# An attention and expert kernel: filler products on a program constant, score banks filled one behind the other, four value copies turned into transfers, two groups of transposes swapped

## The chip, the cores and the metric

The kernel runs on one core of a Trainium2 chip. The metric is the device time of one execution in microseconds. The engines are named as the profile names them: PE is TensorE (PEld its weight loads), DVE is VectorE, ACT is ScalarE, POOL is GpSimd, and SP is SyncE, which issues most of the transfers.

## The reference

```
q, k, v: (4, 8, 576, 64)
scores = q @ k^T / 8, masked to 0 <= query - key < 64; attention = softmax @ v
x = attention as (2304, 512)
logits = x @ w_gate + log1p(exp(x @ w_noise)) * noise; the two best of 8 experts, softmax weights
out = sum over the two of weight * (relu(x @ w1[e]) @ w2[e])        # w1 (8,512,1024), w2 (8,1024,512)
h = out @ w_in;  g = h if h >= 1, 0 if h <= -1, else (h + 1)^2 / 4;  result = g @ w_out
```

## The kernel before, in words

The program is one long sequence in an order written out by hand, and every engine takes its own instructions strictly in that order. Three parts follow one another: attention with routing (to about 104 us), the eight experts, and the second network. Only the first is touched.

Attention works on 18 tiles of 128 tokens. A tile i consists of two units, u = 2i and 2i + 1. Unit k of a tile uses rows 64k to 64k + 63 of the transposed queries and keys, which holds one head of each of four pairs. These are the pieces, by the names in the code:

- `A(i)` computes the scores of both units of tile i on TensorE: for each unit two mask products into the unit's bank (64x512, opening it), and eight score products (64x128), two for each of four head pairs. Unit u has bank `Sb[u % 3]`, unit 3 a bank of `OB`.
- `top(u)` takes the maximum of the scores on VectorE (a reduction of 128x512) and negates and scales it, on VectorE for u < 4 and on POOL behind that. `soft(u)` is four exponentials on ScalarE. `C(u)` transposes the result on TensorE, and ScalarE copies it out as `pt`.
- `Dm(u)`, for odd u, multiplies a whole tile with the values: 16 products, 64x65, of `vO[i]` and `vE[i]`, into `OB`. VectorE divides by the sums (`rl`, `x`), and SyncE stores the tile to `x_dram`.
- `Ex(i, u)` transposes tile i of `x`, and `logits` multiplies it with the gate's weights. `route(g)` for groups of 8, 4 and 6 tiles is a list of small VectorE operations that is played out in portions between the attention's own (`advance`), with one-hot rows (`ohr`, `ohe`) that `place` multiplies on TensorE.

`step(u)` for u = 0 to 36 puts them in order: loads, `A` of the tile after next (even u), `Ex`, `C(u)`, `top`, `soft`, `logits`, `place`, `advance`, `Dm(u - 1)`. The transposes of `C` and `Ex` take turns in two banks (`rot`). In step 34 before the change `C(34)` came ahead of `Ex(15, 34)`.

Two small overlaps between neighbours matter here. A tile's keys reach 64 tokens back: `load_qk(j)` loads queries and keys for a pair of tiles, keys into columns 64 to 319 of a buffer, and `keys_before(j)` copies the 64 before them, on POOL, from the pair before. The values do the same: `vO[i + 1]` is the buffer `vE[i]`, and after tile i's products its first 64 rows are overwritten with those of `vE[i + 1]`, by a POOL copy in `Dm` (L415).

At the very start TensorE fills the time until the first queries and keys are there: `open_ids` opens the bank in which the places of tokens are collected, and `warm(9)` makes nine products of 128x512 of the zero tile `wz`, which VectorE sets first. Four more follow behind the first scores.

All loads, and the stores of tiles, go through SyncE's one queue, in the order of the program.

Of the kernel before, what the change touches and what calls it, by code (L numbers as in the profile page):

```python
# [13 lines left out]
BF16 = mybir.dt.bfloat16  # L14
# [7 lines left out]
P = 128  # L22
# [6 lines left out]
NT = N // P  # L29
# [28 lines left out]
def fused_kernel(ctx, tc, qT, kT, v, wg, noise, wcat, out, wd=None):  # L58
    nc = tc.nc
# [26 lines left out]
    OB = att.enter_context(tc.tile_pool(name="pso", bufs=1, space=PS)).tile([P, 2, 512], F32, name="ob")  # L86


    kTv = kT.rearrange("(g p) t -> p g t", p=P)
    qTv = qT.rearrange("(g p) t -> p g t", p=P)  # L90
    k_t, vE, vO = {}, {}, {}
# [9 lines left out]
    def load_qk(j):  # L101
        q_t[j] = qbuf[:, j % 2]
        kt = k_t[j] = qk.tile([P, 4, 320], F32, tag="k", name=f"k{j}")

        for h in (slice(0, P), slice(P, 256)) if j == 0 else (slice(0, 256),):
            t = slice(256 * j + h.start, 256 * j + h.stop)
            nc.sync.dma_start(out=kt[:, :, 64 + h.start:64 + h.stop], in_=kTv[:, :, t])
            nc.sync.dma_start(out=q_t[j][:, :, h], in_=qTv[:, :, t])
        if j == 0:
            nc.vector.memset(kt[:, :, 0:64], 0.0)  # L110


    def keys_before(j):
        nc.gpsimd.tensor_copy(k_t[j][:, :, 0:64], k_t[j - 1][:, :, 256:320])
# [18 lines left out]
    def load_raw(n, eng=nc.sync):  # L133
        raws[n] = t = raw.tile([P, 1024], F32, tag="raw", name=f"raw{n}")
        if NF <= n < N2:

            if n % NF == 0:
                r = E - 2 if n >= NCE else (n // NF - 1) % (E - 2)
                dyn[n // NF] = nc.values_load(cnt_i[0:1, 1 + r:2 + r], engines=[mybir.EngineType.SP], min_val=0,
                                          max_val=(E - 1) * NF)  # L140
            eng.dma_start(out=t, in_=wcat[bass.ds(dyn[n // NF] + n % NF, 1)].rearrange("o p n -> (o p) n"))
        else:
            eng.dma_start(out=t, in_=wcat[n])
# [184 lines left out]
    NU = 2 * NT  # L328
# [6 lines left out]
    def rot(u):  # L335
        turn[0] += 1
        return bank[3 + 2 * (turn[0] % 2)] if u <= NU else bank[6]
# [6 lines left out]
    def score(u):  # L344
        return OB[:, 0, :] if u == 3 else Sb[u % 3]

    def A(i):
        j = i // 2
        qo, ko = (i % 2) * P, (i % 2) * P
        sb = [score(2 * i + k) for k in range(2)]  # L350
        for k in range(2):
            r = slice(64 * k, 64 * k + 64)
            for c in range(2):
                m = masks[c][int((2 * i + c) % 9 == 0)]
                nc.tensor.matmul(sb[k][64 * c:64 * c + 64, :], lhsT=id64[r, :],
                                 rhs=m[r].unsqueeze(1).to_broadcast([64, 4, P]), start=True, stop=False)
        for g in range(4):
            for c in range(2):
                for k in range(2):
                    r = slice(64 * k, 64 * k + 64)  # L360
                    keys = k_t[j][r, g, ko + 64 * c:ko + 64 * c + P]
                    if c == 0:
                        keys = keys.rearrange("p (s n) -> p s n", s=2)[:, ::-1, :]
                    nc.tensor.matmul(sb[k][64 * c:64 * c + 64, g * P:g * P + P],
                                     lhsT=q_t[j][r, g, qo + 64 * c:qo + 64 * c + 64],
                                     rhs=keys, start=False, stop=(g == 3))

    def top(u):
        mx = wk.tile([P, 4], F32, tag="mx", name=f"mx{u}", bufs=3)
        nb = wk.tile([P, 4], F32, tag="nb", name=f"nb{u}", bufs=3)  # L370
        nc.vector.tensor_reduce(out=mx, in_=score(u).rearrange("p (g n) -> p g n", g=4), axis=AX.X, op=ALU.max)

        (nc.vector if u < 4 else nc.gpsimd).tensor_scalar(out=nb, in0=mx, scalar1=-0.125, scalar2=None, op0=ALU.mult)
        mxs[u] = nb

    def soft(u):
        sb, nb = score(u), mxs.pop(u)
        p = wk.tile([P, 4, P], F32, tag="p", name=f"p{u}", bufs=4)
        for g in range(4):
            nc.scalar.activation(p[:, g, :], sb[:, g * P:g * P + P], AF.Exp, bias=nb[:, g:g + 1], scale=0.125)  # L380
        pr[u] = p

    def C(u):
        p = pr.pop(u)
        PTb = rot(u)
        for g in range(4):
            nc.tensor.transpose(PTb[:, g * P:g * P + P], p[:, g, :], idn)
        t = wk.tile([P, 512], F32, tag="pt", name=f"pt{u}", bufs=PTB)
        nc.scalar.activation(t, PTb, AF.Copy)
        pts[u] = t  # L390

    def Dm(u):
        i, r = divmod(u, 2)
        if r == 0:
            return
        ts = [pts.pop(2 * i + k) for k in range(2)]
        for h in range(H):
            g, k = divmod(h, 2)
            for c in range(2):
                vv = (vO, vE)[c][i]  # L400
                nc.tensor.matmul(OB[64 * c:64 * c + 64, h // 4, (h % 4) * VW:(h % 4) * VW + VW],
                                 lhsT=ts[k][:, g * P + 64 * c:g * P + 64 * c + 64], rhs=vv[:, h * VW:h * VW + VW],
                                 start=True, stop=True)
        ov = OB[:, :, 0:4 * VW].rearrange("p b (h d) -> p b h d", d=VW)
        rl = wk.tile([P, 2, 4, 1], F32, tag="rl", name=f"rl{i}")
        nc.vector.tensor_scalar(out=rl, in0=ov[:, :, :, D:VW], scalar1=1e-9, scalar2=None, op0=ALU.add)
        nc.vector.reciprocal(out=rl, in_=rl)
        x = wk.tile([P, H, D], F32, tag="x", name=f"x{i}", bufs=3)
        nc.vector.tensor_tensor(out=x.rearrange("p (b h) d -> p b h d", b=2), in0=ov[:, :, :, 0:D],
                                in1=rl.to_broadcast([P, 2, 4, D]), op=ALU.mult)  # L410
        xs[i] = x
        nc.sync.dma_start(out=x_dram[P * i:P * i + P, :], in_=x.rearrange("p h d -> p (h d)"))
        if i + 1 < NT:
            if i + 2 < NT:
                nc.gpsimd.tensor_copy(vE[i][0:64, :], vE[i + 1][0:64, :])  # L415
            vO[i + 1] = vE[i]

# [236 lines left out]
    def warm(n, to=OB[:, 1, :]):  # L654
        for _ in range(n):
            nc.tensor.matmul(to, lhsT=wz[:, 0:P], rhs=wz, start=True, stop=True)

    def open_ids():
        nc.tensor.matmul(IDS[:, 0:2 * NK], lhsT=wz[:, 0:P], rhs=wz[:, 0:2 * NK], start=True, stop=False)

    open_ids()
    warm(9)
    A(0)
    for u in range(2):
        top(u)
        soft(u)
    warm(4)

    def logits(i, u):
        Gm(i, u)  # L670
        g, t = tile_group[i]
        if t == GROUPS[g] - 1:
            live.append(route(g))
            next(live[-1])

    def step(u):
        for c in range(EW):
            if u == L0 + LS * c:
                load_raw(c)
        if u + 2 < NU:  # L680
            if (u + 2) % 4 == 0 and (u + 2) // 4 + 1 < NT // 2:
                load_qk((u + 2) // 4 + 1)
                keys_before((u + 2) // 4 + 1)
            if (u + 1) % 2 == 0 and (u + 1) // 2 + 1 < NT:
                load_v((u + 1) // 2 + 1)


        m = u // 2
        if u % 2 == 0:
            if u + 2 < NU:  # L690
                A(m + 1)
            if u == NU:
                nc.scalar.activation(vE[NT - 2][0:64, :], vE[NT - 1][0:64, :], AF.Copy)
            if u == NU - 2:
                C(u)
            if 0 <= m - 2 < NT:
                Ex(m - 2, u)
        if u < NU and u != NU - 2:
            C(u)
        if u % 2 == 0 and u + 2 < NU:  # L700
            top(u + 2)
            top(u + 3)
        if u + 2 < NU:
            soft(u + 2)

        if u % 2 == 1 and 0 <= m - 2 < NT:
            logits(m - 2, u)
        place()
        early()
        advance(MARKS[u > NU - 10])  # L710
        if 0 <= u - 1 < NU:
            Dm(u - 1)

        for c in range(EW):
            for h in range(2):
                if u == L0 + LS * c + 3 + h:
                    split_w(c, h)
                if u == L0 + LS * c + 4 + h and c < EW - 2:
                    rest_w(c, slice(512 * h, 512 * h + 512))
            if u == L0 + LS * c + 4 and EW <= c + 2 < NF:  # L720
                load_raw(c + 2)
# [694 lines left out]
    for q, (ui, p) in enumerate(items):  # L1416
# [5 lines left out]
        while ndone < len(items) and ndone <= q + (1 if items[ndone][0] == FIRST2 else 2):  # L1422
            i = items[ndone]
# [84 lines left out]
```

## Time and profile before

| | us |
|---|---|
| median of 3 runs | 947.14 (946.4 to 947.47) |
| the profiled execution, its time | 950.02 |
| its span (first to last instruction) | 948.3 |
| busy in it: TensorE | 935.7 |
| VectorE | 665.6 |
| ScalarE | 436.5 |
| POOL | 186.2 |

The profiled execution is one of its own and carries the profiler; its time is compared with its span, and differences with the median. Busy time is a share over stages of different kinds: which engine sets the pace of a stage is read from that stage.

### The profile page before, as it was taken

What the parts mean: (1) busy time and instruction counts of PE and PEld (TensorE: products, weight loads), DVE (VectorE), ACT (ScalarE), POOL (GpSimd) and SP (SyncE); (2) the same over time, 40 slices, a digit from 0 to 9 for tenths busy, and PEclk for the clock granted to TensorE, in tenths of its full rate; (3) what the DMA queues carried; (4) which work ended last, traced back from release to release, by engine and by line L of the source; (5) the groups of instructions that cost most, each with busy time, mean ns of one, the idle gap of its engine ahead of it and who ended that gap; (6) DMA issues with size and microseconds to landing.
All of it is one profiled execution on the core that took longest, in us unless ns stands there. A gap on an engine that the chain in (4) does not pass through costs nothing. (4 is left out here: it accounts for less than half of the span.)

```text
span 948.3 us, 17990 instructions
## 1 busy us (share of the span) xinstructions
PE 935.7 (99%) x6779; PEld 832.3 (88%) x6781; DVE 665.6 (70%) x1411; ACT 436.5 (46%) x907; POOL 186.2 (20%) x249
## 2 busy tenths in 40 slices
PE   9999999999999999999999999999999999999998
PEld 6887888988888989898888889988999899899986
DVE  4689765477997968889533366767867776687664
ACT  6898314345565555555433266333433333342221
POOL 3222013133645353354402030000000000000000
PEclk9999999999999999999999999999999999999999
DMA  8874136555888878767725566775576559556521
GB/s 258 300 252 167 56 100 186 188 191 199 290 288 275 261 236 277 257 206 260 252 89 184 204 231 236 252 256 178 177 256 213 164 174 308 175 178 213 182 95 44
DMA packets 91274, 196.95 MB, mean 208 GB/s; under 512 B 7320, under 2 KB 18072, under 8 KB 91184
## 3 DMA queue, kind: packets, MB, share of 16 engines
q1 hardware_dynamic: 83152, 171.68, 54.6%
q0 software_dynamic: 6736, 21.86, 6.4%
q10 hardware_dynamic: 1296, 2.23, 0.6%
q8 instruction: 54, 0.88, 0.4%
q14 instruction: 36, 0.29, 0.1%
HBM read 155.45 MB, written 40.29 MB: 206 GB/s over the span
## 5 line engine op out<-in xcount | busy, mean ns | idle before, releaser
L969 PE MATMUL bank<-wo,hall 128*128 128x512 f32 x864 | 237.6, 394 | 0.0
L969 PE MATMUL bank<-w,hall 128*128 128x512 f32 (+3 forms) x944 | 234.6, 396 | 0.1
L969 PEld LDWEIGHTS bank<-w,hall 128*128 128x128 f32 (+3 forms) x944 | 167.7, 183 | 35.2 <-issue 0.3
L969 PEld LDWEIGHTS bank<-wo,hall 128*128 128x128 f32 x864 | 146.7, 188 | 17.4 <-DVE hall L915 0.2
L904 ACT ACTIVATE hall<-bank 128x288 fp32r<-128x288 f32 (+6 forms) x128 | 54.0, 422 | 218.4 <-PE bank L896 200.6
L896 PE MATMUL bank<-xhie,w 128*128 128x288 f32 (+4 forms) x768 | 122.5, 302 | 0.3 <-DVE hall L907 0.2
L896 PEld LDWEIGHTS bank<-xhie,w 128*128 128x128 f32 x768 | 113.5, 188 | 7.1 <-DVE hall L907 1.4
L907 DVE SCALAR_TENSOR_TENSOR hall<-bank,hall 128x288 fp32r<-128x288 f32 (+7 forms) x168 | 60.0, 391 | 82.5 <-ACT hall L904 75.1
L149 DVE TENSOR_TENSOR w<-raw,w 128x1024 fp32r<-128x1024 f32 (+1 forms) x69 | 81.9, 1188 | 23.8 <-ACT w L158 17.8
L1183 PEld LDWEIGHTS bank<-xb,wi 128*128 128x128 f32 x576 | 80.8, 188 | 8.4 <-DVE cg L1173 0.7
L1207 ACT ACTIVATE hall<-cg 128x512 fp32r<-128x512 f32 x64 | 40.3, 629 | 100.4 <-DVE cg L1205 100.4
L1183 PE MATMUL bank<-xb,wi 128*128 128x256 f32 x576 | 84.3, 282 | 0.3 <-DVE cg L1173 0.3
L1183 PEld LDWEIGHTS bank<-xc,wi 128*128 128x128 f32 x480 | 67.5, 188 | 6.5
L1183 PE MATMUL bank<-xc,wi 128*128 128x256 f32 x480 | 69.9, 280 | 0.0
L158 ACT ACTIVATE w<-raw 128x1024 fp32r<-128x1024 f32 (+1 forms) x71 | 69.4, 977 | 0.0
L896 PE MATMUL bank<-xloe,w 128*128 128x288 f32 (+4 forms) x384 | 69.0, 301 | 0.0
L1201 ACT ACTIVATE mg<-cg 128x512 f32<-128x512 f32 x64 | 40.1, 626 | 45.8 <-DVE cg L1173 44.1
L204 POOL TENSOR_TENSOR td<-rawd 128x512 f32<-128x512 f32 x32 | 33.3, 1040 | 139.6 <-DVE rawd L202 111.8
L896 PEld LDWEIGHTS bank<-xloe,w 128*128 128x128 f32 x384 | 58.0, 188 | 0.0
L1202 DVE SCALAR_TENSOR_TENSOR cg<-mg,cg 128x512 f32<-128x512 f32 x64 | 43.8, 684 | 18.8 <-ACT mg L1201 18.8
L1211 DVE SCALAR_TENSOR_TENSOR hall<-cg,hall 128x512 fp32r<-128x512 f32 x64 | 44.0, 687 | 8.1 <-ACT hall L1207 7.7
L1205 DVE SCALAR_TENSOR_TENSOR cg<-mg,cg 128x512 f32<-128x512 f32 x64 | 44.0, 687 | 1.0
(285 smaller groups left out, 1389.2 us busy)
## 6 DMA issues: line engine op xcount, KB each, us to landing
wi<-w1o SPq DMA_DIRECT2D x56, 1024.0 KB
raw<-wcat SPq DMA_DIRECT2D x64, 512.0 KB
rawd<-wd SPq DMA_DIRECT2D x32, 512.0 KB
w1o<-so SPq DMA_DIRECT2D x64, 256.0 KB
y<-y_dram SPq DMA_DIRECT2D x28, 256.0 KB
vE<-v SPq DMA_DIRECT2D x18, 260.0 KB
x_dram<-x SPq DMA_DIRECT2D x18, 256.0 KB
k<-kT SPq DMA_DIRECT2D x8, 512.0 KB
```

The source lines that it names most:

```text
L149: nc.vector.tensor_tensor(out=w[:, 1, c], in0=t[:, c], in1=w[:, 0, c].bitcast(F32), op=ALU.subtract)
L158: nc.scalar.activation(w[:, 0, c], t[:, c], AF.Copy)
L896: nc.tensor.matmul(ps, lhsT=l[k], rhs=r[:, k, s:s + w], start=(c == 0), stop=(c == len(prods) - 1))
L904: nc.scalar.activation(hh, ps, AF.Relu)
L907: nc.vector.scalar_tensor_tensor(out=t, in0=ps[:, c], scalar=0.0, in1=hh[:, c].bitcast(F32), op0=ALU.max, op1=ALU.subtract)
L969: nc.tensor.matmul(M2[b][0:w], lhsT=h2[:, o:o + w], rhs=r[n], start=(first and a == 0), stop=(last and a == end))
L1183: nc.tensor.matmul(ps, lhsT=w[:, l, k * P:k * P + P], rhs=r[:, m, k, :], start=(c == 0), stop=(c == len(prods) - 1))
L1201: nc.scalar.activation(st["m"], c, AF.Relu, scale=0.5)
L1202: nc.vector.scalar_tensor_tensor(out=c, in0=st["m"], scalar=1.0, in1=c, op0=ALU.min, op1=ALU.subtract)
L1205: nc.vector.scalar_tensor_tensor(out=c, in0=st["m"], scalar=1.0, in1=c, op0=ALU.min, op1=ALU.mult)
L1207: nc.scalar.activation(h2[:, 0:T], c, AF.Copy, scale=-1.0)
L1211: nc.vector.scalar_tensor_tensor(out=h2[:, T:2 * T], in0=c, scalar=-1.0, in1=h2[:, 0:T].bitcast(F32), op0=ALU.mult, op1=ALU.subtract)
```

## The change

Four things are changed.

1. The nine filler products at the start take both operands from a program constant (bf16 1.0, read again and again) instead of the tile `wz`, and stand ahead of `open_ids`.
2. `A(0)` is split: all of unit 0's score products, then its `top` and `soft` in the program, then unit 1's. For the other tiles nothing is changed in `A`.
3. For tiles 12 to 15 the first half of the next values is loaded into `vE[i]` by a transfer from `v` instead of being copied on POOL; and the last key load (j = 8) brings its 64 columns before itself, so its POOL copy is dropped.
4. In step 34 `C(34)` stands behind `Ex(15, 34)`, as in all other steps.

```diff
         for h in (slice(0, P), slice(P, 256)) if j == 0 else (slice(0, 256),):
             t = slice(256 * j + h.start, 256 * j + h.stop)
-            nc.sync.dma_start(out=kt[:, :, 64 + h.start:64 + h.stop], in_=kTv[:, :, t])
+            b = 64 if j == NT // 2 - 1 else 0
+            nc.sync.dma_start(out=kt[:, :, 64 + h.start - b:64 + h.stop], in_=kTv[:, :, t.start - b:t.stop])
             nc.sync.dma_start(out=q_t[j][:, :, h], in_=qTv[:, :, t])
...
-    def A(i):
+    def A(i, ks=(0, 1)):
...
-        for k in range(2):
+        for k in ks:
...
-                for k in range(2):
+                for k in ks:
...
         xs[i] = x
+        if 12 <= i < NT - 2:
+            nc.sync.dma_start(out=vE[i][0:64, :], in_=v[P * i + P:P * i + P + 64, :])
         nc.sync.dma_start(out=x_dram[P * i:P * i + P, :], in_=x.rearrange("p h d -> p (h d)"))
         if i + 1 < NT:
-            if i + 2 < NT:
+            if i < 12:
                 nc.gpsimd.tensor_copy(vE[i][0:64, :], vE[i + 1][0:64, :])
             vO[i + 1] = vE[i]
...
+    one = nc.const_aps.tensor(1.0, [P, 512], BF16)
+    for _ in range(9):
+        nc.tensor.matmul(OB[:, 1, :], lhsT=one[:, 0:P], rhs=one, start=True, stop=True)
     open_ids()
-    warm(9)
-    A(0)
     for u in range(2):
+        A(0, (u,))
         top(u)
         soft(u)
     warm(4)
...
-                keys_before((u + 2) // 4 + 1)
+                if (u + 2) // 4 + 2 < NT // 2:
+                    keys_before((u + 2) // 4 + 1)
...
-            if u == NU - 2:
-                C(u)
             if 0 <= m - 2 < NT:
                 Ex(m - 2, u)
-        if u < NU and u != NU - 2:
+        if u < NU:
             C(u)
```

Where instructions stand now. First TensorE, from its first instruction on; `bank_73` and `bank_74` are the score banks of units 0 and 1, `bank_78` the bank of the places, `k_112` and `qbuf` the first keys and queries. Before (of the fillers one is shown, and of alternating products the first two):

```order
L659 LDWEIGHTS wz
L659 MATMUL bank_78<-wz 128x290
L656 LDWEIGHTS wz
L656 MATMUL ob<-wz 128x512
...
L355 MATMUL bank_73<-mask_135,id_132 64x512
...
L355 MATMUL bank_74<-mask_136,id_132 64x512
L364 MATMUL bank_73<-k_112,qbuf 64x128
L364 MATMUL bank_74<-k_112,qbuf 64x128
```

The same place in the changed kernel:

```order
L666 LDWEIGHTS const-bfloat16-1.0
L666 MATMUL ob<-const-bfloat16-1.0 128x512
...
L662 LDWEIGHTS wz
L662 MATMUL bank_78<-wz 128x290
...
L356 MATMUL bank_73<-mask_135,id_132 64x512
...
L365 MATMUL bank_73<-k_112,qbuf 64x128 x8
...
L356 MATMUL bank_74<-mask_136,id_132 64x512
L365 MATMUL bank_74<-k_112,qbuf 64x128 x8
```

The fillers moved ahead of the first product that reads `wz`, and unit 0's eight score products ahead of unit 1's masks.

Then SyncE at the last key and query load; `x_1556` (`x_1555` in the changed kernel) is tile 12, `vE_1560` (`vE_1559`) the values of tile 15. Before:

```order
L143 DMA raw_1476<-wcat 128x1024
L107 DMA k_1478<-kT 128x4x256
L108 DMA qbuf<-qT 128x4x256
L412 DMA x_dram<-x_1556 128x512
L121 DMA vE_1560<-v 128x520
```

The same place in the changed kernel:

```order
L144 DMA raw_1476<-wcat 128x1024
L108 DMA k_1478<-kT 128x4x320
L109 DMA qbuf<-qT 128x4x256
L414 DMA vE_1213<-v 64x520
L415 DMA x_dram<-x_1555 128x512
L122 DMA vE_1559<-v 128x520
L414 DMA vE_1321<-v 64x520
```

The key load is wider, and a half value load stands ahead of the store of tile 12 and of each of the three after it. On POOL the copies are gone, and nothing else has moved there.

## Rows read from the trace of the kernel before

**Rows 1.** The table by stage; columns in its second line.
```profile
core 0 of [0], span 948.3 us
core 0: us, PE busy (x) PEld busy (x) DVE busy (x) ACT busy (x) POOL busy (x), PEclk, DMA share, GB/s
...
30.00:40.00 10.00, 10.00 (x204) 8.99 (x203) 6.70 (x15) 8.93 (x28) 2.44 (x7) 1.00 0.81 275
...
75.00:80.00 5.00, 4.73 (x92) 4.02 (x90) 4.86 (x22) 5.00 (x16) 1.13 (x3) 1.00 0.64 226
...
200.00:948.00 748.00, 743.65 (x4580) 666.10 (x4578) 531.59 (x990) 321.63 (x612) 137.65 (x132) 1.00 0.64 214
```

**Rows 2.** Timeline, first 12 us: start, duration, engine, operation [idle before, releaser].
```profile
0.79 1.28 ACT L253 ACT_TABLE_LOAD   x1 [0.79 <-PEq L1500]
1.25 0.42 PE L659 MATMUL bank<-wz 128*128 128x290 bf16 x1 [1.25 <-DVE wz L95]
1.47 4.05 PE L656 MATMUL ob<-wz 128*128 128x512 bf16 x9
5.87 1.06 PE L364 MATMUL bank<-k,qbuf 64*64 64x128 f32 x32
6.39 0.40 POOL L114 COPY k<-k 128x256 f32<-128x256 f32 x1 [2.19 <-DMA k<-kT]
6.99 0.69 DVE L371 TENSOR_REDUCE mx<-bank 128x4 f32<-128x512 f32 x1 [4.63 <-PE bank L364]
8.13 2.17 ACT L380 ACTIVATE p<-bank,nb 128x128 f32<-128x128 f32 x8 [6.05 <-DVE nb L373]
11.88 0.40 PE L355 MATMUL bank<-mask,id 64*64 64x512 bf16 x2 [0.85 <-ACT p L380]
```

**Rows 3.** Timeline of POOL, the copy behind tile 12.
```profile
71.75 0.61 POOL L415 COPY vE<-vE 64x520 f32<-64x520 f32 x1 [0.19 <-POOL nb L373]
```

**Rows 4.** Timeline of VectorE, 71 to 90 us.
```profile
71.73 0.70 DVE L593 TENSOR_SCALAR ohe<-io,rf 128x145 f16<-128x145 f16 x1
...
78.86 0.16 DVE L406 TENSOR_SCALAR rl<-ob 128x8 f32<-128x8 f32 x1
...
82.02 1.28 DVE L371 TENSOR_REDUCE mx<-bank 128x4 f32<-128x512 f32 x2
...
83.69 0.60 DVE L543 TENSOR_TENSOR ohs<-o 128x32 bf16<-128x32 f32 x1
...
89.33 1.17 DVE L586 TENSOR_SCALAR ohr<-io,rf,tcode 128x128 f16<-128x128 f16 x3
```

**Rows 5.** Three of these lines by themselves; durations in ns, least, median, longest.
```profile
L593 DVE TENSOR_SCALAR ohe<-io,rf x12: 250/258/697, 71.3 to 90.8; 128x145 f16<-128x145 f16 x12
L586 DVE TENSOR_SCALAR ohr<-io,rf,tcode x24: 301/309/716, 69.4 to 90.6; 128x128 f16<-128x128 f16 x24
L543 DVE TENSOR_TENSOR ohs<-o x3: 209/226/605, 65.9 to 111.5; 128x64 bf16<-128x64 f32 x1, 128x32 bf16<-128x32 f32 x1, 128x48 bf16<-128x48 f32 x1
```

**Rows 6.** Timeline of SyncE's issues, 70 to 74 us.
```profile
70.48 0.65 SPq L108 DMA_DIRECT2D qbuf<-qT  x1
73.48 0.34 SPq L412 DMA_DIRECT2D x_dram<-x  x1
```

**Rows 7.** Transfers in total, in 0 to 4.9 us and in 71.7 to 78.2.
```profile
DMA packets 1558, 0.78 MB, mean 158 GB/s; under 512 B 43, under 2 KB 1558, under 8 KB 1558
DMA packets 1629, 2.38 MB, mean 367 GB/s; under 512 B 104, under 2 KB 1127, under 8 KB 1628
```

**Rows 8.** Timeline of TensorE, 75 to 94 us.
```profile
75.59 1.15 PE L401 MATMUL ob<-vE,pt 128*64 128x65 f32 x32
...
80.13 0.63 PE L422 MATMUL bank<-idn,x 128*128 128x128 f32 x4
...
88.43 1.15 PE L401 MATMUL ob<-vE,pt 128*64 128x65 f32 x32
...
93.46 0.16 PE L612 MATMUL bank<-Cn,ones 128*128 128x1 bf16 x1 [0.57 <-DVE first L479]
```

## The prediction

> **What bounds the kernel now.** I began with the table by stage [rows 1]. From 200 us on TensorE is busy for 743.65 of 748 us and from 30 to 40 us for 10.00 of 10. With so little idle time, what it gains or loses before is kept to the end. Two places differ. From 75 to 80 us it is busy for 4.73 of 5 us while VectorE has 4.86 of 5: routing of finished tiles is mixed into the attention there, and VectorE sets the pace. The other is the start, read next in the order of time [rows 2]: TensorE waits 1.25 us for a memset, and at 11.88 it waits 0.85 us for ScalarE's exponentials, which began at 8.13 when the first negated maximum was there. Then I read VectorE between 68 and 93 us [rows 4, 5] and, beside it, POOL [rows 3], and last what stands in SyncE's queue there [rows 6] and how many bytes the queue moved [rows 7].
>
> The profiled execution took 950.02 us, 1.7 more than its span of 948.3. It lies 2.9 above the median of 947.14; I make the differences in the span and put them onto the median.
>
> **The start.** The nine filler products no longer read wz, so they no longer wait for VectorE. The constant is written ahead of the release that lets all engines go; ScalarE, let go by the same release, starts at 0.79 [rows 2]. So TensorE can start between 0.79 and 1.25; I take 0.85, a gain of 0.40. The fillers have the same shape and number, so the first scores come at 5.87 - 0.40 = 5.47. Is their data there? They need the first two transfers, 256 KB each. The first three (0.786 MB) had moved by 4.9 us [rows 7], and POOL's copy that waits for the third starts at 6.39 [rows 2]: 1.49 us from the last byte to the waiting engine. The third's 0.262 MB take 0.7 us at 0.367 MB/us [rows 7], so the second is usable by 5.7 at the latest. That is an upper bound, and at worst 0.2 of the 0.40 is lost to it.
>
> Unit by unit: before, both units' score passes alternate, 32 records in 1.06 us, and VectorE starts its first reduction at 6.99, after the last. Now unit 0's 16 come alone. They take half of 1.06 if what is issued sets the pace, all of 1.06 if each unit's own stream does. Unit 0 is ready at 6.0 to 6.5, and VectorE starts 0.4 to 0.9 earlier. ScalarE at 8.13 waits for exactly this, and TensorE at 11.88 for ScalarE; from there TensorE is dense. Against it, unit 1's mask products and passes now lie behind, so the next tile's scores may come later: by nothing in the first case, by 0.6 us or more in the second, where they would hold back ScalarE's third unit and the term turns into a loss of 0.2. The mask products speak for the first: the nine fillers end at 1.47 + 4.05 = 5.52, the scores start at 5.87, and in these 0.35 us go four products of 512 columns, of which a filler takes 0.45 for one. Products on different quarters of the array do run side by side. So I lean to the first case: **-0.7 us**, between -0.9 and +0.2.
>
> **What POOL's copies cost.** They look free, since POOL idles. But VectorE's rows next to them are stretched: with the copy at 71.75 [rows 3] an operation of 0.258 takes 0.70; with the later ones 0.226 becomes 0.60, and of three that take 0.309 each one takes 0.716 [rows 4, 5]. That is 0.44, 0.38 and 0.41 us on the engine that sets the pace. Four value copies removed at a mean of 0.41 are 1.6 us if nothing else comes. The removed key copy is not counted (0 to one more such stretch).
>
> **What the transfers bring.** The first late half (tile 12) can be issued when tile 12's value products are done, which is when POOL's copy started: 71.75. The next tile's value products need it at 75.59 [rows 8]. In SyncE's program it stands right behind the last key and query loads; the query load was issued at 70.48 [rows 6]. From 71.7 to 78.2 the queue moved 2.38 MB at 0.367 MB/us [rows 7]. Of these the tile store issued at 73.48 [rows 6] and the value load behind it (0.528 MB by their shapes) came later; 1.85 MB stood ahead. The wider key load adds 0.131 MB and the half itself is 0.133: 2.11 MB at 0.367 MB/us is 5.7 us, so its last byte moves at about 77.4, and with 1.49 us it is usable at 78.9. This rests on transfers being served in the order of issue; POOL's copy at 6.39, which fits three transfers in turn, speaks for it.
>
> The Trainium skill (DMA: Bandwidth & Descriptors, Queues, rings and completion order) says that each DMA engine consumes descriptors in ring order. By that rule, which the 6.39 row agrees with, a small late transfer can't overtake the 1 MB ahead of it; if it could, the sum would be the 944.8 of the second case below.
>
> So TensorE stands at these products from 75.59 to 78.9, some 3.3 us, and queued behind them are the next transposes, logits and scores. They end at 78.9 + 1.15 = 80.05 instead of 76.74. VectorE came to the result at 78.86 before [rows 4]; now it is 1.2 late, and what the removed copies up to there had saved is lost in this wait. Does it get worse? From the end of these products to that of the next scores TensorE had 76.74 to 80.13 = 3.4 us [rows 8], VectorE from 78.86 to its next reductions at 82.02 3.2 us [rows 4]: 0.2 more. Behind it the copies near 83.7 and 89.8 are gone: 0.38 + 0.41 = 0.8 back. The later halves find a queue that has run dry; at 1.49 us plus 0.133 MB they need about 2 us, and from the end of one tile's products (88.43 + 1.15 = 89.58) to the start of the next at about 93.55 there are 4 [rows 8]. At 93.46 TensorE waits for VectorE [rows 8], so what remains there is passed on: 1.2 + 0.2 - 0.8 = **+0.6 us**. Bounds: the half usable by 76.9 (then nothing waits: -1.6), or a microsecond later than worked out (+1.5).
>
> **The last edit** swaps the transposes of unit 34 and of tile 15. Both lie ahead of the row at 93.46, where TensorE idled 0.57 us for VectorE: nothing, by that cover. Without it, the tile's transposes come 0.5 us sooner or later.
>
> **Sum.** -0.7 + 0.6 + 0 = -0.1: 947.14 - 0.1 = 947.0 us.
>
> **Rivals.** *The halves come in time*, because transfers overlap or the queue is shorter than before. Then -0.7 - 1.6 = -2.3, 944.8 us. For it: the rows of VectorE are plain, and the gain needs only that the half is usable by 76.9. Against it: 1.85 MB ahead in a queue that moves 0.37 per us. Chance 0.28.
>
> *TensorE's clock falls in the wait*, the case on the other side. At the start, after idling, the fillers' 512 columns go by every 0.43 to 0.45 us (nine in 4.05 [rows 2]), the pace of the lower level, 1.2 GHz, and it lasted from 1.25 to about the first scores at 5.87. If the same 4.6 us of half pace followed the new wait, they would cost 2.3 us: -0.1 + 2.3, 949.3 us. Against it: the wait is spread over less than the idle before a kernel, and no such wait of 3 us stands in the rows; the longest here, 0.85 at 11.88, is shorter. It decides from 4.0 us of half pace on, which cost 2.0. Chance 0.10. The Trainium skill (TensorE: Matmul & The Clock Gate, Part 1: The HAM clock gate) says that an idle TensorE goes back to 1.2 GHz; no row here shows it in mid-kernel.
>
> *The change of the start does not do what it says*: one unit alone takes as long as two, and the start term is +0.2 instead of -0.7. With the wait: 947.14 + 0.2 + 0.6 = 947.9. The mask products speak against it. Chance 0.12. The forecast itself: 0.50.
>
> **Range and chances.** A measurement of this kernel can tell about 0.2% (1.9 us) from no change: 945.25 and 949.03 are the borders. Faster: the first rival (nearly all) and a little of the forecast, where the half lands a microsecond early: 0.30. Slower: the clock: 0.10. Same: 0.60. The range takes in the first rival down to 944.5 (its -2.3 with 0.3 more at the start) and upward the weak start with a transfer later by 0.9, 948.8. The forecast's own range is 946.0 to 948.2.
>
> **What the new profile would show.** First filler product at about 0.85, VectorE's first reduction at about 6.3, ScalarE's first exponential about 0.7 before 8.13, the idle row of masks near 11.2. No VectorE operation of 0.7 us where 0.26 is usual after tile 12. A wait of TensorE of about 3 us at the value products (128x65) near 75 us, released by a DMA, and VectorE waiting after it: that is the step on which most hangs. If there is no such wait, the second case holds. If products behind it are twice as far apart, the third.

## The result, and the profile after

| | before | after |
|---|---|---|
| median, us | 946.85 (946.4 to 947.47, 6 runs) | 952.97 (950.46 to 953.48, 6 runs) |
| the profiled execution, its time | 950.02 | 952.68 |
| its span | 948.3 | 951.0 |
| first product of the experts starts at | 103.73 | 109.04 |

The measured ratio is 1.0061 [1.0048, 1.0074], which is 5.8 us [4.5 to 7.0]; the medians differ by 6.1 us. The changed kernel is slower, outside the forecast range of 944.5 to 948.8. That the two profiled spans differ by 2.7 only has a reason behind the changed part. The profile of before stands once among the experts, in its timeline of TensorE:

```profile
153.98 0.54 PE L761 MATMUL bank<-idr,xge 128*128 128x128 f32 x4 [2.16 <-DVE xloe L768]
```

The profile after has no such wait. What the change did is therefore read before the experts begin: their first product comes 109.04 - 103.73 = 5.3 us later, before and then after:

```profile
103.73 1.66 PE L896 MATMUL bank<-xhi0a,w 128*128 128x384 f32 x8
```
```profile
109.04 1.66 PE L900 MATMUL bank<-xhi0a,w 128*128 128x384 f32 x8
```

(Line numbers after are a few higher: the value products are L402, the scores L365, `rl` L407.)

TensorE's longest wait shows where: 4.6 us at the value products, released by the half transfer of values (its row, at 80.55, stands below). The next longest are the two at the start, 0.9 and 0.8. The table by stage, with the columns of [rows 1], shows what the wait did and what followed:

```profile
75.00:80.00 5.00, 0.99 (x11) 0.76 (x8) 3.63 (x17) 3.68 (x12) 0.45 (x2) 1.00 1.00 307
80.00:85.00 5.00, 4.45 (x48) 4.15 (x48) 1.32 (x7) 1.85 (x7) 0.00 (x0) 0.62 0.34 116
85.00:90.00 5.00, 5.00 (x82) 4.23 (x81) 4.13 (x24) 2.59 (x8) 0.44 (x2) 0.70 0.16 52
```

From 75 to 80 us TensorE is busy for 0.99 of 5 us, while the DMA engines are busy all the time (share 1.00). Then the granted clock, still 1.00 in that stage, is 0.62 and 0.70, and from 90 us on 1.00 again. Of 10 us, (0.38 + 0.30) x 5 = 3.4 us of full pace are missing; as there are only two levels, TensorE ran for 6.8 us at 1.2 GHz instead of 2.4. The fall came not with the wait but some 0.6 us into the products behind it: the clock is 1.00 from 80.50 to 81.00 us and 0.58 from 81.00 to 82.00. TensorE's own timeline shows what that costs. The transposes of `C` are L388, those of `Ex` L425, logits L443:

```profile
80.55 1.51 PE L402 MATMUL ob<-vE,pt 128*64 128x65 f32 x32 [4.56 <-DMA vE<-v]
81.99 1.12 PE L388 MATMUL bank<-idn,p 128*128 128x128 f32 x4
82.90 1.73 PE L443 MATMUL bank<-wg_sb,xt 128*128 128x16 f32 x8
...
85.48 1.92 PE L365 MATMUL bank<-k,qbuf 64*64 64x128 f32 x32
87.33 0.95 PE L425 MATMUL bank<-idn,x 128*128 128x128 f32 x4
...
88.90 1.15 PE L402 MATMUL ob<-vE,pt 128*64 128x65 f32 x32
...
99.04 0.16 PE L615 MATMUL bank<-Cn,ones 128*128 128x1 bf16 x1 [0.16 <-DVE first L482]
```

The same groups of products in the same trace, at full pace, take 1.15 (88.90), 0.65 (L388 at 71.85), 0.96 (L443 at 72.34), 1.04 (L365 at 73.61) and 0.65 (L425 at 74.58). The five groups lose 0.36 + 0.47 + 0.77 + 0.88 + 0.30 = 2.8 us. The row that stood at 93.46 [rows 8] is at 99.04, 5.6 later.

VectorE, which set the pace here before, now waits for TensorE:

```profile
82.11 0.17 DVE L407 TENSOR_SCALAR rl<-ob 128x8 f32<-128x8 f32 x1 [3.40 <-PE ob L402]
...
84.74 0.17 DVE L446 COPY lgs<-bank 128x16 f32<-128x16 f32 x1 [1.50 <-PE bank L443]
...
87.53 1.29 DVE L372 TENSOR_REDUCE mx<-bank 128x4 f32<-128x512 f32 x2 [0.56 <-PE bank L365]
...
89.20 0.19 DVE L546 TENSOR_TENSOR ohs<-o 128x32 bf16<-128x32 f32 x1
...
95.32 0.75 DVE L589 TENSOR_SCALAR ohr<-io,rf,tcode 128x128 f16<-128x128 f16 x3
```

The result of the products is read at 82.11, before at 78.86 [rows 4]. The last two lines are operations that POOL's copies had stretched: 0.19 against 0.60, 0.75 for three against 1.17 [rows 4].

Why the half comes late is seen in SyncE's issues, and in the total of the transfers from 71.7 to 79.2 us:

```profile
70.47 0.43 SPq L108 DMA_DIRECT2D k<-kT  x1
70.96 0.50 SPq L109 DMA_DIRECT2D qbuf<-qT  x1
71.99 0.48 SPq L414 DMA_DIRECT2D vE<-v  x1
```
```profile
DMA packets 1530, 2.36 MB, mean 314 GB/s; under 512 B 91, under 2 KB 1109, under 8 KB 1529
```

The half was issued at 71.99, right behind the keys and queries, and released the products at 80.55: 8.6 us for 0.133 MB. The queue moved 0.314 MB per us, before 0.367 [rows 7].

The start, TensorE first, then VectorE's first reduction:

```profile
0.84 4.00 PE L666 MATMUL ob<-const-bfloat16-1.0 128*128 128x512 bf16 x9 [0.84 <-PEq L1504]
...
5.01 0.64 PE L356 MATMUL bank<-mask,id 64*64 64x512 bf16 x2
5.44 1.02 PE L365 MATMUL bank<-k,qbuf 64*64 64x128 f32 x10
6.20 0.40 PE L356 MATMUL bank<-mask,id 64*64 64x512 bf16 x2
6.29 1.18 PE L365 MATMUL bank<-k,qbuf 64*64 64x128 f32 x22
...
11.96 0.40 PE L356 MATMUL bank<-mask,id 64*64 64x512 bf16 x2 [0.95 <-ACT p L381]
```
```profile
6.83 0.69 DVE L372 TENSOR_REDUCE mx<-bank 128x4 f32<-128x512 f32 x1 [4.47 <-PE bank L365]
```

The fillers start 0.41 earlier and the first scores 0.43, at 5.44. But the first reduction is only 0.16 earlier than at 6.99, and the masks that closed the start at 11.88 [rows 2] are 0.08 later.

### The profile page after: what moved, and what is told of

Same layout as the page of the kernel before. It is cut to its first block, busy times and chain, and to the rows that moved or that the text cites. A ratio compares the mean times of both kernels' runs of the same rounds, so it can differ in the third digit from the quotient of the medians.

```text
span 951.0 us, 17993 instructions
## 1 busy us (share of the span) xinstructions
PE 938.1 (99%) x6781; PEld 835.7 (88%) x6781; DVE 665.5 (70%) x1411; ACT 437.2 (46%) x907; POOL 183.3 (19%) x244
## 5 line engine op out<-in xcount | busy, mean ns | idle before, releaser
L911 DVE SCALAR_TENSOR_TENSOR hall<-bank,hall 128x288 fp32r<-128x288 f32 (+7 forms) x168 | 59.9, 391 | 78.9 <-ACT hall L908 78.2
```

The costliest lines, as they stand in the source:

```text
L911: nc.vector.scalar_tensor_tensor(out=t, in0=ps[:, c], scalar=0.0, in1=hh[:, c].bitcast(F32), op0=ALU.max, op1=ALU.subtract)
```

## The experiments

Twelve kernels were run, in three sets, each beside the kernel before on the same chip. The changed kernel itself was timed only in the set of the result above. On the first set's chip the kernel before took 951.1 us, beside the second and third set 947.3 and 947.2. So the ratios to it are what is compared, each with its 95% interval. All compute the whole reference. The theories: **wait and clock** (the half is late because of the bytes ahead of it; TensorE's wait costs its own length and then a stretch at the lower level), against it **wait alone**, **order in SyncE's queue** (not the bytes, but the place in that one queue), and **the start** (the split of `A(0)` loses the time).

### Which part makes the loss

**no_late** leaves all copies on POOL as before, and keeps the rest of the change.

```diff
-        if 12 <= i < NT - 2:
-            nc.sync.dma_start(out=vE[i][0:64, :], ...)
...
-            if i < 12:
+            if i + 2 < NT:
```

> The changed kernel, but all sixteen value halves copied on POOL as before; fillers, split first scores, wide key load and the swap stay. Theory: the loss of 6.1 us (946.85 to 952.97) comes from the transfer of tile 12's half, for which TensorE waits 4.56 us, and from its granted clock of half behind it, so it goes with the transfer: 946.9, give or take 0.8. Rival: another edit (split scores, wide key load, swap) carries a good part: 949 or more.

Measured: 951.89 us, ratio 1.0007 [0.9998, 1.0016]. The loss is gone with the transfers; they carry 0.61 - 0.07 = 0.54% of it. Its trace shows one thing more. With the wide key load kept, TensorE waits for the last queries, and behind this wait, short as it is, the clock falls too:

```profile
80.63 1.38 PE L365 MATMUL bank<-k,qbuf 64*64 64x128 f32 x32 [0.78 <-DMA qbuf<-qT]
```

From 80 to 85 us it is 0.66, which is 0.34 x 5 x 2 = 3.4 us at the lower level.

**late_only** is the opposite: the kernel before with the four half transfers and nothing else.

```diff
+        if 12 <= i < NT - 2:
+            nc.sync.dma_start(out=vE[i][0:64, :], ...)
...
-            if i + 2 < NT:
+            if i < 12:
```

> The kernel before with nothing changed but the four value halves of tiles 12 to 15 as transfers (no wide key load, no change at the start, no swap). Theory: these alone make the loss: wait of 3.5 to 4.5 us at tile 13's value products, half clock behind it, 951.5 to 953. Rival: the wide key load (1280 bytes a row instead of 1024) makes the queue late; without it the wait is under 2 us and the clock holds: 948 or less.

Measured: 954.11 us, ratio 1.0062 [1.0039, 1.0084], the whole loss and a little more than was expected. TensorE's timeline:

```profile
79.50 1.31 PE L401 MATMUL ob<-vE,pt 128*64 128x65 f32 x32 [3.57 <-DMA vE<-v]
```

and the table by stage behind it:

```profile
80.00:85.00 5.00, 5.00 (x60) 4.46 (x58) 2.58 (x19) 2.75 (x8) 0.00 (x0) 0.53 0.48 137
85.00:90.00 5.00, 5.00 (x78) 4.47 (x71) 3.75 (x14) 2.42 (x7) 0.44 (x2) 0.78 0.00 0
```

Without the wider key load the wait is a microsecond shorter, and the clock falls all the same: (0.47 + 0.22) x 5 = 3.45 us of full pace are missing.

**key_only** is the kernel before with the wider last key load, and its copy on POOL dropped.

```diff
-            nc.sync.dma_start(out=kt[:, :, 64 + h.start:64 + h.stop], in_=kTv[:, :, t])
+            b = 64 if j == NT // 2 - 1 else 0
+            nc.sync.dma_start(out=kt[:, :, 64 + h.start - b:64 + h.stop], in_=kTv[:, :, t.start - b:t.stop])
...
-                keys_before((u + 2) // 4 + 1)
+                if (u + 2) // 4 + 2 < NT // 2:
+                    keys_before((u + 2) // 4 + 1)
```

> The kernel before with nothing changed but the last key load, 640 KB with its own 64 columns instead of 512 KB and a POOL copy. Theory: the query load behind it lands 0.4 us or more later, tile 16's scores wait up to 1 us for it, VectorE wins about 0.3 us at the removed copy: +0.0% to +0.1%. Rival (the prediction's step, which counted only bytes in the backlog): no wait of TensorE for queries, 0.0% or a gain.

Measured: 947.09 us, 0.9996 [0.9988, 1.0005]: no change that can be told. Its trace shows a wait of TensorE of 0.26 us at the scores at 79.92, released by the query load behind the wider keys.

**const_only** has only the fillers on the constant, ahead of `open_ids`.

```diff
+    one = nc.const_aps.tensor(1.0, [P, 512], BF16)
+    for _ in range(9):
+        nc.tensor.matmul(OB[:, 1, :], lhsT=one[:, 0:P], rhs=one, start=True, stop=True)
     open_ids()
-    warm(9)
```

> The kernel before with nothing changed but the nine fillers on the constant, ahead of opening the bank of places. Theory: TensorE starts 0.41 us earlier, but its granted clock rises at 5.9 to 6.1 us from the span's start as in both kernels, so the first scores run at half pace for longer and of the 0.41 some 0.1 to 0.2 are left: 946.7, within noise of 946.85. Rival (the prediction's step): the whole 0.4 is kept to the end: 946.45 or less.

Measured: 947.24 us, 1.0002 [0.9994, 1.0011]. The timeline of its start (TensorE, then VectorE):

```profile
5.01 0.64 PE L355 MATMUL bank<-mask,id 64*64 64x512 bf16 x4
5.43 1.57 PE L364 MATMUL bank<-k,qbuf 64*64 64x128 f32 x32
```
```profile
7.07 0.69 DVE L371 TENSOR_REDUCE mx<-bank 128x4 f32<-128x512 f32 x1 [4.70 <-PE bank L364]
```

The 32 score records start 0.44 earlier and take 1.57 us instead of 1.06 [rows 2]. In this execution the first reduction is no earlier at all: what the fillers gain is lost right behind them. But it is one execution, and the moment of full pace differs between executions. In the trace of late13_int (below), with the same fillers, the same masks already run at full pace:

```profile
5.00 0.41 PE L356 MATMUL bank<-mask,id 64*64 64x512 bf16 x4
```

With fillers on `wz` it differs as much: these masks take 0.41 at 5.10 in late13_only's trace, and the scores behind them 1.70 at 5.88 in key_only's. So one trace against another cannot tell what the 0.40 is worth, and in the median no gain can be told.

**split_only** has only unit 0's scores ahead of unit 1's.

```diff
-    def A(i):
+    def A(i, ks=(0, 1)):
...
-    A(0)
     for u in range(2):
+        A(0, (u,))
         top(u)
         soft(u)
```

> The kernel before with nothing changed but the first tile's scores unit by unit. Theory: a unit alone takes nearly as long as both together (in the changed kernel 0.75 us of starts for unit 0 against 0.79 for both), so VectorE starts 0.1 to 0.3 earlier, unit 1 and the next tile's scores come 0.5 later, and ScalarE's third unit is where it was or 0.2 later: 946.9 to 947.1. Rival (the prediction's step): a unit alone takes half: 946.5 or less.

Measured: 948.26 us, 1.0012 [1.0001, 1.0023]: a loss of some 1.1 us where 0.3 at most was expected, its interval just clear of none. Its timeline:

```profile
5.87 0.76 PE L365 MATMUL bank<-k,qbuf 64*64 64x128 f32 x10
6.37 0.40 PE L356 MATMUL bank<-mask,id 64*64 64x512 bf16 x2
6.47 1.18 PE L365 MATMUL bank<-k,qbuf 64*64 64x128 f32 x22
```
```profile
7.01 0.69 DVE L372 TENSOR_REDUCE mx<-bank 128x4 f32<-128x512 f32 x1 [4.64 <-PE bank L365]
```

Both units together had taken 1.06 from 5.87 [rows 2]. Now they take until 6.47 + 1.18 = 7.65, and VectorE starts its first reduction at 7.01 against 6.99. One unit's stream takes nearly as long as both side by side. Two traces at full pace from the first mask on say the same: in fill_wait's (split) the first scores start at 5.03 and the reduction at 6.11, 1.08 later; in late13_int's (both units) at 5.24 and 6.35, 1.11 later. This is the third rival of the prediction, the weak start.

The masks that close the start come at 12.14 against 11.88 [rows 2]. That is 0.26 of the 1.1 us. Where the rest goes isn't shown: the first product of the experts comes at 105.50, 1.8 later, but 1.7 us of full pace are missing from 90 to 100 us in this trace (clock 0.97, then 0.69). The clock isn't all of it, since the executions at a mean clock of 1.000 alone have medians of 948.15 (6) against 947.25 (13).

The four parts alone add up to 0.02 + 0.12 + 0.62 - 0.04 = 0.72%; the whole change measured 0.61%, within their intervals.

### Wait, clock and queue

**fill_wait** is the changed kernel with 20 filler products (added work) ahead of tile 13's value products, so that TensorE isn't idle while it would wait.

```diff
         ts = [pts.pop(2 * i + k) for k in range(2)]
+        if i == 13:
+            warm(20)
```

> The changed kernel with twenty filler products of 128x512 (added work, 4.3 us at 0.213 each) ahead of tile 13's value products, that is in the 4.56 us wait. Theory: the transfer lands when it did, but TensorE's granted clock stays at 1.00, and half of the 6.8 us at half clock comes back: 949.6, between 949 and 950.5. Rival: the clock costs nothing because VectorE sets the pace there, or falls all the same: 952.5 or more.

Measured: 953.88 us, 1.0032 [1.002, 1.0044]. The timeline of TensorE and the table by stage:

```profile
75.00 4.26 PE L661 MATMUL ob<-wz 128*128 128x512 bf16 x19
79.19 1.15 PE L404 MATMUL ob<-vE,pt 128*64 128x65 f32 x32
80.27 0.66 PE L388 MATMUL bank<-idn,p 128*128 128x128 f32 x4
80.77 0.96 PE L445 MATMUL bank<-wg_sb,xt 128*128 128x16 f32 x8
...
105.03 1.66 PE L902 MATMUL bank<-xhi0a,w 128*128 128x384 f32 x8
```
```profile
75.00:80.00 5.00, 5.00 (x45) 2.56 (x46) 2.60 (x15) 2.66 (x9) 0.29 (x2) 1.00 0.78 260
80.00:85.00 5.00, 5.00 (x96) 4.44 (x94) 4.23 (x24) 3.84 (x10) 0.19 (x1) 1.00 0.46 136
```

The products still come only at 79.19, yet the clock stays at 1.00, and the groups behind take 1.15, 0.66 and 0.96 where the changed kernel took 1.51, 1.12 and 1.73. This trace runs a microsecond ahead of the changed kernel's already (the half is issued at 70.95, there at 71.99), so what counts is the distance. From the issue to the products it is 8.24 us, there 8.56: the wait is nearly the same. From the products to the first of the experts it is 105.03 - 79.19 = 25.84 us, there 109.04 - 80.55 = 28.49: 2.65 less. In the kernel before it is 103.73 - 75.59 = 28.14. So by these traces 2.30 of the wait are given back when the clock is held (28.14 - 25.84), and the fall of the clock costs 2.65.

The medians agree. Of the 0.61% about half is left, 0.32%. The other 0.29% is 2.7 us, as the 2.65 here and the 2.8 summed over the five slowed groups. The intervals (some 0.13% either way, each) leave the split at 2.7 with about 1.7 either way. "Wait alone" falls.

**pool_queue** issues the same four half transfers from POOL's queue instead of SyncE's.

```diff
-            nc.sync.dma_start(out=vE[i][0:64, :], ...)
+            nc.gpsimd.dma_start(out=vE[i][0:64, :], ...)
```

> The changed kernel with the four half transfers issued by POOL instead of SyncE, same bytes, same moment, another queue. Theory: the half is late because it stands behind the key and query loads in SyncE's own queue; in another queue it lands some 2 to 4 us after its issue near 71.8, in time for 75.6 or nearly so: 945.5 to 947. Rival: it is late because the 16 DMA engines are busy with 2 MB until 78, whichever queue it is in: 949.5 or more, with a wait of 3 us or more at tile 13's value products.

Measured: 961.54 us, 1.0111 [1.0096, 1.0127], the slowest of all. POOL's issue and the products that wait for it:

```profile
72.00 0.77 POOL L414 DMA_DIRECT2D vE<-v  x1 [0.74 <-PE bank L388]
```
```profile
79.26 1.15 PE L402 MATMUL ob<-vE,pt 128*64 128x65 f32 x32 [3.90 <-DMA vE<-v]
```

In a queue of its own the half takes 7.3 us from issue to use. The table of queues (packets, MB, share of the 16 engines) for 73 to 75 us, and then for 75 to 77, shows how:

```profile
q1 hardware_dynamic: 266, 0.60, 85.8%
```
```profile
q1 hardware_dynamic: 507, 0.62, 92.7%
q0 software_dynamic: 22, 0.07, 9.5%
```

POOL's queue (q0) moved nothing before 76 us, then 0.07 MB to 77 and 0.07 more to 79, while SyncE's (q1) moved 0.62 and 0.49 over the same 16 engines. So the place in SyncE's queue alone isn't the cause: in another queue the half is late as well. The Trainium skill (DMA: Bandwidth & Descriptors, Queues, rings and completion order) says that an engine takes turns between the queues that have work for it; the two lines of 75 to 77 agree.

What held POOL's queue until 76 isn't shown: from 73 to 75 the engines were busy for 86%, not all the time. The later three halves, issued at 80.76, 89.16 and 94.86 with little else to move, were moved whole by 83, 91.2 and 97, so POOL does not always need that long to get a transfer going.

Not all of the loss comes from this wait. The clock is at 0.55 and 0.77 from 80 to 85 and 85 to 90 us, and near the end of the attention TensorE waits a second time, 2.29 us at 102.74, for ScalarE; the cause isn't seen.

**early_load** is the changed kernel with the last keys and queries loaded some 6 us sooner, in step 24 behind `A`.

```diff
-            if (u + 2) % 4 == 0 and (u + 2) // 4 + 1 < NT // 2:
+            if (u + 2) % 4 == 0 and (u + 2) // 4 + 1 < NT // 2 - 1:
                 load_qk((u + 2) // 4 + 1)
...
                 A(m + 1)
+            if u == 24:
+                load_qk(NT // 2 - 1)
```

> The changed kernel with the last key and query loads (1.15 MB) issued one step pair earlier, behind the scores of tile 13 in step 24, so that they no longer stand ahead of tile 12's half. Theory: the half was late only because of the bytes ahead of it, whichever queue it is in; with 1.15 MB fewer it is usable up to 3 us earlier, the wait at tile 13's value products falls from 4.56 us to 1.5 or less, TensorE's granted clock stays at 1.00, and the loss against before falls from 0.6% to between -0.1% and +0.2%. Rival: a half value transfer of 64 rows takes some 8 us on its own account: wait of 4 us or more, loss of 0.5% or more.

Measured: 946.95 us, 1.0003 [0.9991, 1.0015]. SyncE's queue, and TensorE's timeline:

```profile
64.20 0.38 SPq L108 DMA_DIRECT2D k<-kT  x1
...
71.85 0.48 SPq L414 DMA_DIRECT2D vE<-v  x1
```
```profile
77.20 1.15 PE L402 MATMUL ob<-vE,pt 128*64 128x65 f32 x32 [1.36 <-DMA vE<-v]
```

The half is issued as before at 71.85 in the same queue, but with 1.18 MB less ahead of it; TensorE waits 1.36 us instead of 4.56, the products behind take 1.15 again, and the loss is gone. The bytes ahead are the cause, in whichever queue the half stands.

### Where the transfers would do

**late13** starts them one tile later (13 in place of 12), where no load of keys is ahead.

```diff
-        if 12 <= i < NT - 2:
+        if 13 <= i < NT - 2:
...
-            if i < 12:
+            if i < 13:
```

> The changed kernel with the transfers from tile 13 on (three instead of four); tile 12's half copied on POOL. Theory: only tile 12's half stands behind the key and query loads (issued 71.99, products released at 80.55), the other three found a queue that had run dry, so there is no such wait, VectorE gains 0.28 + 0.38 + 0.41 at the three removed copies, and the sum is 946.85 + 0.1 (start) - 1.0 = 945.9. Rival: any half value transfer comes late by itself (64 rows, next needed one tile later): 949 or more, with a wait of TensorE at the value products of a later tile.

Measured: 951.16 us, 0.9997 [0.9988, 1.0006]: no wait for values, no loss, and no gain that can be told where 1.0 us was expected. In its trace, as in no_late's, TensorE waits for the last queries (0.97 us at 81.50), and the clock is at 0.66 from 80 to 85 us.

**late13_only** is the kernel before with these three transfers alone.

```diff
+        if 13 <= i < NT - 2:
+            nc.sync.dma_start(out=vE[i][0:64, :], ...)
...
-            if i + 2 < NT:
+            if i < 13:
```

> The kernel before with nothing changed but the value halves of tiles 13 to 15 as transfers. Theory: VectorE is rid of three stretches (0.28, 0.38, 0.41 us) in a stage where it sets the pace, and nothing waits: -1.1 us, -0.11%. Rival: the stretches cost nothing at the end: within 0.03% of before.

Measured: 946.79 us, 0.9993 [0.9983, 1.0004]. The point agrees with a gain from VectorE's unstretched operations, the interval includes none: inconclusive. The executions at a mean clock of 1.000 alone speak for the gain: medians of 946.09 (6) against 947.12 (24), 1.0 less where 1.1 was expected. They were picked out after the fact.

**early_load_int** is early_load with the first scores alternating as before.

```diff
+    A(0)
     for u in range(2):
-        A(0, (u,))
         top(u)
```

> As early_load, and the first tile's scores alternate again between the two units. Theory: the sum of the good parts; against before -0.15% to -0.35%, 0.1 to 0.2% under early_load, which is what the split of the first scores costs. Rival: the split costs nothing once the wait is gone: equal to early_load.

Measured: 945.96 us, 0.9991 [0.9979, 1.0003], with a wait of 1.97 us at 77.58 that is still there. Better than early_load by 0.12%, what split_only lost, though within the intervals, and against before less than the 0.15% expected at least.

**late13_int** joins what cost nothing: fillers on the constant, alternating first scores, transfers from tile 13, the wider key load, the swap. Its edit is that of late13 and this last one together.

> The changed kernel with the transfers from tile 13 on and the first tile's scores of both units alternating again: constant fillers, wide key load, three half transfers, swap. Theory: the best of the parts: 945.5 to 946.0, a little under the one with split scores. Rival: the parts are worth nothing when TensorE sets the pace: 946.8.

Measured: 945.67 us, 0.9981 [0.9973, 0.999]: faster than before by 0.19%, and the best of all. The first value products that need a transferred half, those of tile 14, in TensorE's timeline:

```profile
82.39 1.15 PE L402 MATMUL ob<-vE,pt 128*64 128x65 f32 x32
```

They don't wait, nor do those behind them at 88.07 and 92.79. (The scores at 79.93 wait 0.63 us for the last queries; the clock stays at 1.00.) The first product of the experts starts at 102.54, 1.2 us earlier than before.

### The clock of every run

Each execution's record gives its mean granted clock, so the clock theory can be tried on runs that left no trace.

| kernel | runs, by mean granted clock: us |
|---|---|
| before (second set) | 13 at 1.000: 947.25 median; 10 at 0.999: 946.84; 5 at 0.998: 947.97; 2 at 0.997: 949.53 |
| after | one at 0.998: 950.46; five at 0.994 to 0.996: 952.68 to 953.48 |
| late_only | 0.998: 949.68; 0.997: 949.70; 0.996: 951.21; 0.995: 954.11; 0.994: 954.32; 0.992: 955.51; 0.990: 956.80 |
| early_load | 9 at 0.999 and 1.000: 945.21 to 948.51; 0.997: 948.20; two at 0.996: 950.27 and 951.44 |
| pool_queue | 0.996 (the profiled one): 956.74; four at 0.989: 961.35 to 962.80 |

In late_only a clock lower by 0.008 goes with 7.1 us; 0.008 of 950 us are 7.6 us of full pace. Within most kernels the longer runs are those with the lower clock. It also tells why pool_queue's median lies 5 us above its trace: 0.996 - 0.989 is 6.7 us of full pace over 955. Which wait lowered the clock in those four is not seen, as they left no trace.

## Why the prediction was wrong, step by step

**Forecast 947.0, no change; measured 952.97, slower.** The likeliest case fell; the two mechanisms on which the loss rests both stood in the text, one mis-sized, the other as a rival at 0.10.

*The wait at tile 13's value products*: right in place, releaser and cause (early_load), and mis-sized. I had 3.3 us, it was 4.56. At 0.314 MB per us, which the queue moved, my 2.11 MB take 6.7 us instead of 5.7: usable at 79.9 instead of 78.9. The remaining 0.65 to 80.55 I can't assign; the query load ahead was issued 0.48 later than before (70.96 against 70.48 [rows 6]), which may be part of it. The rate of the trace before was that of another mix of transfers.

*What it costs behind*: this is the step that failed. I let VectorE be 1.2 late, add 0.2 and get 0.8 back from the copies, +0.6 in all. The sum took the products behind the wait at full pace; a lower clock stood in it at nothing, only as a rival. VectorE came to the result at 82.11, 3.25 late, 2.05 more than I had: some 1.25 from the longer wait, 0.36 from the value products themselves at the slow pace, and 0.40 by which TensorE was late already (80.55 - 75.59 is 4.96, the wait 4.56). Behind it nothing was given back: from there to the row at 99.04 another 2.3 were added, because the products that VectorE then waited for ran at half pace (2.8 us over five groups). With the clock held, the step would nearly have stood: of a wait of 3.3 I had 2.7 given back in all (3.3 - 0.6), and fill_wait gives back 2.30. VectorE, on which I let the chain run, waited 3.40, 1.50 and 0.56 us for TensorE.

*The rival of the clock* had this mechanism and nearly this price: 2.3 us for 4.6 us at the lower level, measured 2.7 to 2.8 for 6.8 us. Two reasons stood against it, that the wait was spread over less than the idle before a kernel and that no such wait stood in the rows. The second is no evidence against; it only says that the rows can't tell. The first doesn't hold: 4.56 and 3.57 us in a dense stretch were enough. The Trainium skill (TensorE: Matmul & The Clock Gate, HAM oscillation — how this bites in real kernels) describes products that start at the low level behind each wait for a transfer; the trace agrees in the main, 1.00 ahead of the wait and 0.62 behind it, though here the products' first 0.6 us still ran at 1.00. fill_wait's 1.00 shows that here the idling did it.

*The start*, -0.7: wrong, about +0.1 in the trace at 11.96. Its first half, the fillers' 0.40, was right to 0.01 and brought nothing that can be told: scores that begin at 5.43 take 1.57 instead of 1.06 in const_only's trace. The masks show the pace in the changed kernel: 0.64 for the pair at 5.01, 0.40 at 6.20. Full pace came late in these two executions and early in others with the same fillers (late13_int, fill_wait), so I had counted on a moment that I can't forecast. Its second half, a unit alone in half the time, was wrong by nearly all of it (split_only). I had argued from the mask products in the 0.35 us ahead of the scores; those belong to both units and four quarters of the array, the scores of one unit don't.

*VectorE's stretched operations*: right. They are back at 0.19 and 0.75 [rows 4], and so is the operation of 0.70 at 71.73, now 0.26 at 72.05. What it is worth in time: late13_only's 0.07% (0.7 us, not told from nothing).

*The halves in time* (944.8) is what late13_int comes near to by avoiding the load of keys: 945.67. *The swap* and *the wider keys* cost and bring nothing that can be told: key_only 0.9996 [0.9988, 1.0005]; the swap was not tried alone.

The sum as it should have been, to the first product of the experts: start and drift 0.40, wait 4.56, clock 2.65, less 2.30 that fill_wait gives back (VectorE's slack and its unstretched operations, not measured apart): 5.3. The 5.8 [4.5 to 7.0] of the ratio agree. The forecast of -0.1 lies 5.4 below this sum: 2.65 from the clock, 1.26 from the longer wait, 1.1 from the start and drift (-0.7 against 0.40) and 0.4 given back less.

## What to carry to other kernels

A transfer that replaces an on-chip copy of 0.6 us must be priced by the bytes that are ahead of it at its issue, on all queues: here 8.6 us behind a load of keys and queries, and no wait at all one tile later. A wait of 3 to 5 us on TensorE is to be priced with the stretch of half pace behind it, which here cost another 60% of the wait; where such a wait can't be avoided, filler products keep the pace. A gain of 0.4 us ahead of TensorE's rise to full pace can't be counted on: the moment of that rise differed between executions by more.

## What the runs showed of the hardware

- Behind waits of 4.56 and 3.57 us in a dense stretch the granted clock was at its lower level for 6.8 and 6.9 us; behind waits of 1.36 (early_load) and 1.97 (early_load_int) it stayed at 1.00. The mean clock of most runs of late_only and after is lower than of nearly all of before.
- The length of one wait doesn't settle it. Behind waits of 0.78 and 0.97 us for queries (no_late, late13) the clock was at its lower level for 3.4 us, and behind 0.63 (late13_int) it stayed. Among the experts a wait of 2.17 us (no_late, at 155.68) had 0.66 from 155 to 160 us around and behind it, and one of 2.16 (before, at 153.98) had 1.00. On the first set's chip the kernel before ran 10 of 24 times at a mean of 0.996 or 0.998, without a trace. What decides stays open.
- A half of 0.133 MB in another queue took 7.3 us, against 8.6 in the full queue; with little else to move the same transfer from POOL was done some 2 us after its issue. A queue of its own helped little while SyncE's moved 0.6 MB in 2 us.
- Score products of 64x64 of one unit (16 records) took nearly as long as those of two units side by side (32 records in 1.06 us): at full pace 1.08 against 1.11 us from the first score to the reduction.
- When TensorE reaches full pace at the start differs between executions: with the same fillers the masks near 5.0 us took 0.41 in one trace and 0.64 in another.
